# Attention and a two-layer MLP on one core: queries on partitions 0-63, keys on 64-127, transposes and scores on 64-row halves, key tiles of 120, masks multiplied

## The chip, the cores and the metric

The kernel runs on one core of one Trainium2 chip. The metric is the device time of one execution in microseconds; lower is better. An execution that the hardware profiler recorded gives, beside its time, the start and end of every instruction on the engines: PE (TensorE: matmuls, with PEld for its weight loads), DVE (VectorE), ACT (ScalarE), POOL (GpSimd) and SP (SyncE, which issues DMAs here). ACT and POOL issue DMAs too. A "q" behind an engine's name (SPq) is its sequencer, which issues.

## The reference, cut to what matters

`q`, `k`, `v` are [4, 8, 768, 64] in fp32 (batch, head, token, dimension). Heads 0, 2 and 6 are "retrieval" heads with a full causal mask; the other five are "stream" heads, which see the first 4 keys and a window of 64.

```
scores = scale * np.matmul(q, k.transpose(0, 1, 3, 2))
stream_keep = causal & (is_sink | in_win)      # n_sink = 4, window = 64
mask   = causal for retrieval heads, stream_keep for stream heads
a      = softmax(where(mask, scores, -1e9))
x      = (a @ v) as [3072, 512]                # heads side by side
h      = x @ w_in                              # [3072, 2048]
out    = (max(h, 0) + alpha * min(h, 0)) @ w_out    # [3072, 512]
```

## The kernel before, in words

**Segments.** The 32 heads are worked off in 16 segments `n`, two heads `hh` each: four segments per batch, with the head pairs of `PAIRS` = (2, 6), (1, 5), (0, 4), (3, 7). So n = 0, 4, 8, 12 hold two retrieval heads, n = 2, 6, 10, 14 one retrieval and one stream head, the others two stream heads. The MLP works on token tiles `t` (two per batch, 512 and 256 tokens): P1 (`w_in`, L510), relu on ACT (L515) and prelu on DVE (L522), P2 (`w_out`, L530), and output rows by way of `ot`.

**The order is written out.** `ORDER` (L14-72) lists every step by name; the loop at L672 emits them one after the other, and each engine's queue runs its own instructions in that order. Names: L load, C cast to bf16, T transpose, t copy of the transposed q or k out of PSUM, S scores, s exp, m mask multiply, A attention times V, a normalise, X and x transpose of the result and its copy, P p g O o the MLP, wi and wo weight loads, warm dummy matmuls. Segments n = 0 to 3 (batch 0) come ahead of the MLP: this is called the ramp here. From then on attention of the next batch is mixed with the MLP of the one before.

**Loads.** q and k of one head are 192 KB, on 128 partitions with six token rows each (L186, L189: packets of 1,536 bytes). V of a retrieval head goes to 128 partitions (L201). V of a stream head is laid out in seven overlapping key tiles: KEYS = 124 keys on partitions 4 to 127 (L206), and the four sink keys on partitions 0 to 3 of every tile (L209), in packets of 256 bytes. All of these are issued by SP in their order, but for one k load on ACT. The weights are issued by POOL with a cast (L576, L580).

**From load to scores.** Each head's q and k are cast to bf16 (L276, 128x384 each), most on POOL, in its queue's order. Pairs of bf16 dimensions are taken as one fp32 word and transposed on PE, three 128x128 transposes for q and three for k of a segment (L308). `put_q` copies q to `qT` (128 rows: head 0 on rows 0-63, head 1 on 64-127), `put_k` copies each head's keys to its own `kT`, whose other 64 rows are zero (filled at the start). Because of those zeros a score matmul can use all 128 rows (L352 in batch 0, L362 later). From n = 4 on, scores wait in a list `burst`; when both heads have at least SPLIT = 576 columns in it, they are issued in 64-row form instead, alternating between the halves (L369).

**Masks.** In batch 0 the mask is added inside PE's accumulation: a matmul of an identity with a table of 0 and -30000 (L400, L430). From n = 4 on, the exponentials are multiplied by a 0/1 mask on DVE (L415 `mr` for retrieval heads, L450 and L453 `ms` for stream heads).

**After the scores.** ACT takes the exponential into `eR` or `eS` (L407, L441, L444); PE multiplies with V and a column of ones (L467); DVE normalises into `xn` (L476, L477); three fp32 transposes per segment (L485) and a DVE copy (L490) put the result into `xT`, which P1 reads.

Of the kernel before, what the change touches and what calls it, by code (L numbers as in the profile page):

```python
# [14 lines left out]
busy Lq0.0 warm4 kz0 warm5 one nms id Lk0 zero nmr Lq0.1 Lk3 warm0 warm8 Cq0.1 Ck0.0 Tk0.0 Cq0.0 Tq0.0 kz2 qz0 Tq0.1  # L15
Ck0.1 Ck3.0 nma Tk0.1 Lk1 Lq1 Ck3.1 idb Lk2 tk0.0 kz3 Ck1.1 Ck1.0 warm6 tq0.1 tq0.0 S0.0.1 tk0.1 Tk3 tk3.0 tk3.1
S0.1.1 s0.1.1 warm2 s0.0.1 Cq1 La Tk1 kz1 tk1.0 S0.1.2 sz0 s0.1.2 warm7 Tq1 vo S0.0.0 Lq3 s0.0.0 Ck2.1 S0.1.0 s0.1.0
Ck2.0 Cq3 tq1 S1.0.0 tk1.1 Tk2 S1.1.0 Lv0 s1.0.0 s1.1.0 Tq3 Cv0 Lq2 tq3 S1.1.1 A0.1 m4.0.2 s1.1.1 S0.0.2 s0.0.2 S1.0.1
s1.0.1 Cq2 sz1 tk2.0 Al al Lv1 Cv1 tk2.1 Tq2 wi0 a0.1 wi1 A0.0 a0.0 S3.0.0 A1.0 s3.0.0 S3.0.1 s3.0.1 tq2 vz Lv2 Lv3
A1.1 S3.1.1 s3.1.1 S3.1.0 s3.1.0 S2.0.0 a1.1 a1.0 X1 wi2 S2.0.1 Cv3.0 s2.0.0 x1 sz2 s2.0.1 Cv3.1 wi3 wi7 X0 x0 S2.0.2  # L20
s2.0.2 A3.0 S2.1.0 warm3 s2.1.0 wi6 a3.0 Cv2 A2.0 a2.0 S2.1.1 A3.1 P0.0.0 a3.1 s2.1.1 A2.1 a2.1 P0.1.0 X3 m8.1.2 x3
P0.3.0 m12.1.2 X2 x2 P0.4.0 Lq4 P0.5.0 P0.3.1 Lq5 P0.6 p0.6 m6.0.2 g0.6 P0.1.1 P1.6 P0.0.1 p1.6 Lk4 wi5 P0.3.2 p0.3
g0.3 Cq4 P0.0.2 p0.0 g1.6 P0.5.1 P0.5.2 p0.5 P0.7 g0.5 wi4 P1.2 g0.0 P0.4.1 P0.4.2 p0.4 g0.4 P0.13 Lk5 p0.13 g0.13
p0.7 P1.14 p1.14 P0.14 g1.14 p1.2 P1.0 Cq5 g0.7 Tq4 Ck4.1 p1.0 P0.12 tq4 p0.14 g0.14 P0.1.2 g1.0 P0.2.0 P0.2.1 Ck4.0
Tk4 P1.8 tk4.0 P0.11 tk4.1 P0.2.2 P0.8 Lq6 wo0 g1.2 P1.12 wo1 p0.1 g0.1 p0.11 m4.1.2 p0.12 g0.12 p0.8 g0.8 p1.12
S4.1.4 p1.8 g0.11 s4.1.4 g1.8 P1.10 Ck5.1 Tq5 P0.10 Lk6 p0.10 g0.10 P0.9 tq5 g1.12 P0.15 p0.9 Ck5.0 g0.9 Lk7 Tk5 Ck7.1
p0.15 P1.4 Ck7.0 O1.1.0 Cq6 p0.2 p1.4 O1.0.0 g0.2 O0.2.0 tk5.0 tk5.1 g0.15 O0.0.0 Lq7 Cq7 p1.10 g1.4 Tq6 S4.1.2 s4.1.2
Ck6.0 tq6 g1.10 S4.0.4 O1.0.1 O0.2.1 O1.1.1 wo2 s4.0.4 S4.0.3 S4.1.0 s4.0.3 Tk7 tk7.0 wo3 O0.2.2 O1.0.2 Lv5 tk7.1
s4.1.0 Ck6.1 Tk6 ns Tq7 tq7 O0.0.1 O0.0.2 tk6.0 tk6.1 O0.2.3 S5.1.1 Cv5 s5.1.1 m5.1.1 O0.0.3 o0.2 S5.0.0 S5.1.0 m4.1.4
S5.0.2 S5.1.2 S5.0.1 s5.1.0 m5.1.0 s5.1.2 O1.0.3 S4.1.3 s5.0.1 m5.0.1 s4.1.3 m4.1.0 m4.1.3 O0.3.0 O0.3.1 Lv7 Cv7  # L30
s5.0.2 Lv6 s5.0.0 m5.0.0 S7.0.1 S7.1.0 o1.0 S7.1.2 m5.0.2 S7.0.0 o0.0 A5.0 m5.1.2 s7.0.0 a5.0 s7.0.1 m4.0.3 O1.1.2
A5.1 m7.0.1 S7.0.2 O0.3.2 m4.0.4 s7.1.0 Lk9 Ck9.0 s7.1.2 S4.1.5 S4.0.2 S4.0.0 S4.1.1 s7.0.2 S4.0.1 Ck9.1 O0.3.3 a5.1
s4.1.5 s4.1.1 Lv4 s4.0.1 S7.1.1 s7.1.1 m7.0.0 X5 Cv6 m4.1.5 s4.0.2 m7.0.2 A7.0 s4.0.0 m7.1.0 Cv4 O1.1.3 m4.1.1 S4.0.5
o1.1 a7.0 m4.0.1 O0.1.0 m7.1.2 m4.0.0 x5 s4.0.5 o0.3 S6.0.5 m4.0.5 A4.0 S6.0.1 S6.1.1 m7.1.1 s6.0.1 A7.1 a4.0 S6.0.0
S6.1.0 a7.1 S6.0.3 s6.1.1 A4.1 m6.1.1 Lk8 s6.0.5 S6.1.2 a4.1 s6.0.3 m6.0.3 Ck8.0 Ck8.1 Tk8 Lq9 Lq8 Cq8 O0.1.1 S6.0.4
m6.0.1 S6.0.2 s6.0.0 m6.0.0 X4 s6.1.2 Lk12 m6.1.2 m6.0.5 s6.1.0 s6.0.4 O0.1.2 m6.1.0 A6.1 s6.0.2 m6.0.4 Lv8 x4 a6.1
A6.0 X7 a6.0 O0.1.3 x7 X6 Tq8 Cq9 Tq9 x6 Tk9 P2.1 tq8 Lk10 P2.8 p2.1 g2.1 Lk11 Ck11.1 P2.14 tq9 p2.14 Cv8 P2.5 g2.14
p2.8 g2.8 P2.2 Lq11 P2.9 Lq10 P2.11 tk9.0 p2.2 g2.2 p2.9 g2.9 o0.1 tk8.0 tk8.1 P3.14 tk9.1 P2.12 p2.12 p3.14 Lq12
g3.14 P2.15 Ck10.0 P2.0 p2.11 g2.11 p2.0 Cq10 p2.5 Tq10 tq10 Cq12 g2.12 P2.3 p2.3 g2.0 P2.13 g2.3 p2.13 g2.13 P2.6
P2.7 Lq13 g2.5 p2.7 S8.0.4 s8.0.4 P2.4 g2.7 p2.6 P3.10 g2.6 p3.10 Lq14 p2.4 g2.4 Ck11.0 Tk11 p2.15 Lk15 Cq11 Tq11 P3.2  # L40
g3.10 p3.2 g3.2 P3.8 P3.4 p3.4 g3.4 O2.1.0 p3.8 P2.10 p2.10 P3.6 O2.1.1 g2.10 O2.1.2 g2.15 O2.1.3 Lv11 Cv11 o2.1 Lv9
tk11.0 tk11.1 tq11 p3.6 S8.1.1 s8.1.1 g3.6 P3.12 O2.0.0 g3.8 P3.0 p3.0 O2.0.1 O2.0.2 O2.0.3 g3.0 Lv10 S9.0.0 S9.1.1
S9.1.2 p3.12 g3.12 S9.0.2 S9.0.1 S9.1.0 O2.3.0 O2.3.1 o2.0 s9.0.1 s9.1.0 s9.1.2 s9.1.1 S8.1.5 S8.1.3 S8.0.3 S8.0.1
Ck10.1 Lk14 s9.0.2 s8.1.5 s8.1.3 Tk10 tk10.0 tk10.1 Cq13 Ck12.0 s8.0.1 m8.0.1 m8.1.3 O2.3.2 O2.3.3 S8.1.0 m8.1.1
S8.0.5 s9.0.0 m8.1.5 m9.0.0 S8.0.2 S8.1.2 S8.0.0 S8.1.4 m9.0.2 m10.0.2 m9.1.0 m8.0.4 s8.0.3 m9.1.2 s8.1.0 s8.1.4
m8.1.4 s8.0.2 s8.0.0 s8.0.5 O3.0.0 O3.0.1 S11.1.0 Cv9 O3.0.2 Lv15 m9.1.1 A9.1 m9.0.1 A9.0 s11.1.0 S11.0.0 s8.1.2
s11.0.0 m8.1.0 m8.0.0 O3.0.3 o3.0 m8.0.5 m8.0.3 A8.0 a9.1 S11.1.2 S11.1.1 S11.0.2 S11.0.1 o2.3 s11.0.1 Cv10 A8.1
s11.1.1 s11.0.2 a9.0 X9 a8.0 O3.1.0 a8.1 x9 S10.0.5 S10.1.2 s11.1.2 S10.0.4 S10.1.1 S10.0.0 m11.1.2 O3.1.1 m11.1.1
Ck12.1 Tk12 Lq15 m11.0.1 m11.1.0 s10.1.2 Lk13 s10.1.1 s10.0.0 X8 m10.1.1 Tq12 tq12 m11.0.2 m10.1.2 A11.1 a11.1 O2.2.0
S10.0.1 s10.0.4 Lv12 s10.0.5 tk12.0 tk12.1 O3.1.2 S10.1.0 Ck13.0 S10.0.3 S10.0.2 m10.0.4 m11.0.0 m10.0.5 m10.0.0  # L50
# [12 lines left out]
s14.1.2 s12.0.4 m12.0.4 m12.0.5 S12.1.2 s12.1.2 O4.1.2 S14.1.1 m12.1.4 S14.0.5 m12.1.3 S14.0.3 S14.0.0 S14.0.4 S14.1.0
s14.1.0 m14.1.0 s14.1.1 m14.1.1 A12.0 a12.0 s14.0.3 m14.1.2 s14.0.0 A15.1 m14.0.3 s14.0.5 O4.1.3 A12.1 a12.1 A14.1
a14.1 s14.0.4 m14.0.4 S14.0.1 S14.0.2 s14.0.2 O5.0.0 m14.0.5 s14.0.1 m14.0.0 m14.0.1 O5.0.1 a15.1 A14.0 X12 o4.1 X15
O5.0.2 a14.0 X14 x12 x14 O5.0.3 x15 P6.6 p6.6 P7.0 p7.0 g7.0 o5.0 P7.6 P6.14 P7.8 p6.14 g6.14 P6.12 P6.11 p6.11 g6.11
P7.12 p7.12 g6.6 p7.6 P7.10 P6.8 P6.2 g7.6 P6.10 p6.2 g6.2 p6.12 g7.12 P6.0 p6.10 g6.10 P6.3 p6.3 g6.12 g6.3 P6.7 p6.7
p6.0 g6.0 p7.10 g7.10 g6.7 P6.15 P6.5 P6.1 p6.1 p6.8 p7.8 g6.8 g6.1 g7.8 P6.9 P6.13 P6.4 p6.9 P7.2 p6.13 O6.0.0 p6.15
g6.13 g6.15 O6.1.0 p7.2 p6.4 P7.4 O6.3.0 g6.4 g7.2 O7.0.0 P7.14 p6.5 g6.5 O6.3.1 O6.2.0 O6.2.1 g6.9 O6.2.2 O6.2.3 o6.2
O6.0.1 O6.0.2 O6.0.3 o6.0 O6.3.2 p7.4 O6.3.3 o6.3 g7.4 O6.1.1 O6.1.2 O6.1.3 m12.0.2 o6.1 p7.14 g7.14 O7.0.1 O7.0.2  # L70
O7.0.3 m8.0.2 o7.0 L0 l0 L1 l1 L2 l2 warm1
""".split()


@with_exitstack
def kernel(
    ctx: ExitStack,
    tc: tile.TileContext,
    q: bass.AP,
    k: bass.AP,  # L80
    v: bass.AP,
# [18 lines left out]
    PAIRS = [(2, 6), (1, 5), (0, 4), (3, 7)]  # L100
    NSINK = 4
    NT = 7
    KEYS = 124
    WIDE = KEYS + 64
    SLOT = WIDE + 64
    KEY0 = [64 - KEYS + KEYS * j for j in range(NT)]
# [74 lines left out]
    def rows_in(buf):  # L181
        return buf.rearrange("p h i d -> p h (i d)")
# [530 lines left out]
```

## Time and profile before

| what | value |
|---|---|
| median of 3 runs | 252.78 us (252.49 to 253.58) |
| the profiled execution | 250.98 us |
| its span, first to last instruction | 249.2 us |
| granted TensorE clock, mean | 0.978 |
| PE busy | 234.2 us, 94% |
| DVE busy | 157.3 us, 63% |
| ACT busy | 147.9 us, 59% |
| POOL busy | 58.9 us, 24% |
| DMA | 30.34 MB in 43,374 packets, 28,870 of them under 512 bytes |

A page of the profile shows the span in 40 slices of 6.2 us: a digit is the busy share of a slice in tenths. A matmul's end is modelled and lies behind the start of the next one, so a PE that is busy is not PE at its peak; how far one matmul's start is from the next (its pitch) is read from the chain, the view that follows the work that ended last back to its releasers. Groups of instructions give count, busy time and mean duration. Windows give the busy time of every engine in a stretch, then the granted clock, the DMA share and GB/s.

### The profile page before, as it was taken

How to read it: one execution, taken by the hardware profiler on the slowest of the kernel's cores; microseconds unless marked ns; L12 is line 12 of the kernel's file. 1: busy time of each engine (PE TensorE's matmuls, PEld its weight loads, DVE VectorE, ACT ScalarE, POOL GpSimd, SP SyncE). 2: the span in 40 equal slices, each digit the busy share in tenths (PEclk: the TensorE clock that was granted, in tenths of full speed). 3: DMA queues.
4: the chain of work that ended last, by engine and by line, in shares of the span. 5: the costliest groups of instructions: out<-in, count | busy, mean ns of one | idle time of the engine just before them, and what ended most of it. 6: DMA issues, size and time to landing. Idle time of an engine off the chain costs nothing.

```text
span 249.2 us, 5160 instructions
## 1 busy us (share of the span) xinstructions
PE 234.2 (94%) x1961; PEld 147.0 (59%) x1961; DVE 157.3 (63%) x429; ACT 147.9 (59%) x302; POOL 58.9 (24%) x106
## 2 busy tenths in 40 slices
PE   8996259999999999999999999999999999999995
PEld 7785146666555576557545665575455667455444
DVE  4765125678715996886839894988658663885020
ACT  5584310688999883586477745576569624572231
POOL 4944063820011470340040506200011000000000
PEclk9999957999999999999999999999999999999999
DMA  7946769999337969443553943000021111000132
GB/s 219 313 106 113 123 109 265 317 239 180 63 69 199 316 196 277 173 136 72 129 151 82 281 97 122 1 3 0 1 86 43 45 42 45 0 1 3 42 126 84
DMA packets 43374, 30.34 MB, mean 122 GB/s; under 512 B 28870, under 2 KB 41558, under 8 KB 43350
## 3 DMA queue, kind: packets, MB, share of 16 engines
q1 hardware_dynamic: 37158, 20.70, 29.6%
q0 software_dynamic: 5728, 8.91, 15.5%
q10 hardware_dynamic: 464, 0.40, 0.5%
q8 instruction: 15, 0.25, 0.4%
q14 instruction: 9, 0.07, 0.1%
HBM read 27.92 MB, written 6.29 MB: 137 GB/s over the span
## 4 chain that ended last, share of the span: by engine, by line
PE 77%; SPq 10%; DMA 6%; DVE 4%; POOL 1%; issue 1%; ACT 0%; DVEq 0%
PE P L510 32%; PE P L530 29%; SPq L209 6%; PE P L467 5%; DMA vf<-in_v_dram 5%; PE P L308 3%; PE P L369 3%; PE P L362 2%; DMA kf<-in_k_dram 2%; PE P L485 1%; PE P L547 1%; DVE xn L477 1%; SPq L206 1%; DVE eR L415 1%; SPq L201 1%; SPq L189 1%
## 5 line engine op out<-in xcount | busy, mean ns | idle before, releaser
L522 DVE SCALAR_TENSOR_TENSOR g<-neg,oma,P 128x256 bf16<-128x256 f32 (+1 forms) x128 | 71.1, 610 | 39.2 <-ACT neg L515 38.8
L510 PE MATMUL P<-xT,w_in_b 128*128 128x512 bf16 (+1 forms) x512 | 87.9, 327 | 0.0
L530 PE MATMUL P<-w_out_b,g 128*128 128x512 bf16 x368 | 87.8, 379 | 0.0
L515 ACT ACTIVATE neg<-P 128x512 f32<-128x512 f32 x96 | 54.4, 599 | 36.9 <-PE P L510 32.5
L510 PEld LDWEIGHTS <-w_in_b 128*128 128x128 bf16 x512 | 50.0, 98 | 32.3
L530 PEld LDWEIGHTS <-g 128*128 128x128 bf16 x368 | 34.6, 98 | 34.4 <-issue 1.0
L407 ACT ACTIVATE eR<-P 128x448 bf16<-128x448 f32 (+1 forms) x63 | 34.8, 604 | 6.9 <-PE P L400 3.0
L441 ACT ACTIVATE eS<-P 128x376 bf16<-128x376 f32 (+1 forms) x55 | 26.6, 525 | 20.1 <-PE P L430 10.6
L538 POOL DMA_DIRECT2D out_dram<-ot x18 | 11.4, 632 | 94.7 <-ACT ot L536 94.3
L536 ACT COPY ot<-P 128x512 f32<-128x512 f32 x23 | 13.3, 592 | 24.1 <-PE P L530 22.6
L450 DVE TENSOR_TENSOR eS<-eS,ms 128x376 bf16<-128x376 bf16 x45 | 15.8, 368 | 11.5 <-ACT eS L441 11.3
L477 DVE TENSOR_TENSOR xn<-P,rcp 128x384 bf16<-128x384 f32 x32 | 18.9, 591 | 1.1
L467 PE MATMUL P<-vb,eS 128*128 128x65 bf16 x240 | 11.1, 200 | 8.7 <-POOL vb L296 6.5
L467 PEld LDWEIGHTS <-eS 128*128 128x128 bf16 x240 | 10.1, 102 | 11.4 <-issue 8.7
L276 POOL CAST natk<-kf 128x384 bf16<-128x384 f32 x20 | 12.7, 661 | 9.1 <-DMA kf<-in_k_dram 8.7
L276 POOL CAST natq<-qf 128x384 bf16<-128x384 f32 x20 | 11.5, 623 | 8.8 <-DMA qf<-in_q_dram 5.5
L311 ACT COPY qT<-P 128x768 bf16<-128x768 bf16 (+1 forms) x13 | 10.4, 796 | 4.9 <-PE P L308 4.9
L352 PE MATMUL P<-qT,kT 128*128 128x188 bf16 (+6 forms) x68 | 12.2, 261 | 0.6 <-DVE qT L311 0.5
L467 PE MATMUL P<-vb,eR 128*128 128x65 bf16 x252 | 10.1, 197 | 1.1 <-DVE xT L490 1.1
L415 DVE TENSOR_TENSOR eR<-eR,mr 128x128 bf16<-128x128 bf16 x54 | 10.8, 239 | 0.3 <-ACT eR L407 0.2
L467 PEld LDWEIGHTS <-eR 128*128 128x128 bf16 x252 | 9.3, 100 | 2.7 <-DVE xT L490 1.4
L476 DVE RECIPROCAL rcp<-P 128x6 f32<-128x6 f32 x32 | 6.1, 190 | 7.0 <-PE P L467 6.7
(81 smaller groups left out, 208.2 us busy)
## 6 DMA issues: line engine op xcount, KB each, us to landing
kf<-in_k_dram SPq DMA_DIRECT2D x31, 192.0 KB
qf<-in_q_dram SPq DMA_DIRECT2D x15, 384.0 KB
out_dram<-ot POOLq DMA_DIRECT2D x18, 256.0 KB, 2.8
vf<-in_v_dram SPq DMA_DIRECT2D x19, 217.0 KB
vf<-in_v_dram SPq DMA_DIRECT2D x12, 192.0 KB
w_in_b<-in_moe_w_in_dram POOLq DMA_DIRECT2D x8, 256.0 KB, 7.7
w_out_b<-in_moe_w_out_dram POOLq DMA_DIRECT2D x4, 512.0 KB, 11.9
out_dram<-ot SPq DMA_DIRECT2D x5, 256.0 KB
```

Of the source, the lines that this page charges most:

```text
L209: nc.sync.dma_start(dst[0:NSINK, :, hh, :], dram(v, o, [[D, NSINK], [0, NT], [1, D]]))
L276: copy(in_pairs(nat, hh), buf[:, hh].rearrange("p (i t) d -> p i t d", t=2))
L407: nc.scalar.activation(ebuf[n, hh][:, lo:hi].rearrange("p (x c) -> p x c", x=len(parts)), P[:, got[0]:got[0] + len(parts), 0:(hi - lo) // ...
L441: nc.scalar.activation(slots_of(n, hh, m), sc[:, :, 0:2 * WIDE].rearrange("p x (s c) -> p x s c", c=WIDE), AF.Exp, scale=scale)
L450: nc.vector.tensor_tensor(slots, slots, ms[:, 0:2, :] if m == 0 else ms[:, 1:3, :], op=ALU.mult)
L467: nc.tensor.matmul(pav[:, i, :], e[:, o:o + 128], vv[:, j, hh, 0:D + 1], start=(m == 0), stop=(m == len(terms) - 1))
L477: nc.vector.tensor_tensor(in_pairs(xn[n], hh), pav[:, :, :, 0:D], rcp.to_broadcast([128, 3, 2, D]), op=ALU.mult)
L510: nc.tensor.matmul(psg[:, w * i:w * (i + 1)], w_in_b[:, c, 128 * fb:128 * (fb + 1)], xT[:, c, o:o + w], start=(x == 0), stop=(x == 3))
L515: nc.scalar.activation(neg[t, f], bank(held["P", t, f][0]), AF.Relu, scale=-1.0)
L522: nc.vector.scalar_tensor_tensor(g_buf[t % 2][:, fb, 0:w], neg[t, f][:, c], oma[:, fb:fb + 1], bank(got[0])[:, c], op0=ALU.mult, op1=ALU.add)
L530: nc.tensor.matmul(bank(held["O", t, s][0]), g_buf[t % 2][:, f, 128 * s:128 * (s + 1)], w_out_b[:, f, :], start=(f == 0), stop=(f == 15))
L536: nc.scalar.copy(ot, bank(got[0]))
```

## The change

- q and k of a segment share one buffer `qkf`: q on partitions 0-63, k on 64-127, twelve token rows per partition (packets of 3,072 bytes). Each load fills 64 partitions. One cast instruction takes q and k of a head together (128x768).
- The fp32 transposes work on 64 rows and 64 columns: six for q and six for k per segment, q's on rows 0-63 and k's on 64-127, queued in `burst` and issued alternating between the halves. The result's transposes (X) are halved in the same way, into two adjacent banks.
- `kT` holds both heads one below the other, without the zero halves; only the unused columns are zero-filled. All scores, those of batch 0 too, are 64-row matmuls, whatever the burst's size; SPLIT is gone.
- The masks of batch 0 are multiplied after the exponential, as in the later batches; the PE matmuls with the identity and the tables `nmr` and `nms` are gone.
- KEYS is 120 instead of 124: stream V loads go to 120 partitions, and the key tiles hold 4 + 120 rows.
- Names in `ORDER` can carry an engine (`/P`, `/V`, `/A`): 58 of the 118 mask steps are on POOL (49 of them from n = 4 on), 12 of the 23 output copies that ACT had are on DVE, 8 of 16 x copies on ACT, casts on POOL, DVE and ACT.
- `ORDER` as a whole is another one. Its dummy matmuls stand elsewhere: 25 instead of 3 behind the start of the dense MLP.

The core of the diff (`ORDER` and renamed buffers left out):

```diff
-    KEYS = 124
+    KEYS = 120
...
-    qf = [stat.tile([128, 2, 6, 64], fp32, name=f"qf{i}") for i in range(NF)]
-    kf = [stat.tile([128, 2, 6, 64], fp32, name=f"kf{i}") for i in range(NF)]
+    qkf = [stat.tile([128, 2, 12, 64], fp32, name=f"qkf{i}") for i in range(NF)]
...
-    kT_all = stat.tile([128, NK, 2, 7 * 128], bf16, name="kT")
+    kT_all = stat.tile([128, NK, 7 * 128], bf16, name="kT")
...
+    def load_qk(eng, src, at, n, hs):
+        h = heads(n)[hs[0]]
+        dst = qkf[n % NF][at:at + 64, hs[0]:hs[-1] + 1].rearrange("p h i d -> p h (i d)")
+        dims = [[12 * D, 64], [4 * S * D, len(hs)], [1, 12 * D]]
+        eng.dma_start(dst, dram(src, (n // 4 * H + h) * S * D, dims))
...
-            nc.sync.dma_start(dst[NSINK:128, 0:nt, hh, :], dram(v, o + KEY0[0] * D, [[D, KEYS], [KEYS * D, nt], [1, D]]))
+            nc.sync.dma_start(dst[NSINK:NSINK + KEYS, 0:nt, hh, :], dram(v, o + KEY0[0] * D, [[D, KEYS], [KEYS * D, nt], [1, D]]))
...
+    def cast_qk(n, hh, lo, hi, eng):
+        nat[n] = NAT0[n] if n < 4 else NAT[n % 2]
+        src = qkf[n % NF][:, hh, 2 * lo:2 * hi].rearrange("p (i t) d -> p i d t", t=2)
+        cast_of(eng)(in_pairs(nat[n], hh, 6)[:, lo:hi], src)
...
+    def T_pe(n, key):
+        held["q", key] = take(*ANY)
+        held["k", key] = take(*ANY)
+        words = nat[n].bitcast(fp32).rearrange("p (i c) -> p i c", i=6)
+        c = D if key == "0.0" else 128
+        for i in range(6):
+            for half, x in enumerate((held["q", key][0], held["k", key][0])):
+                r = slice(64 * half, 64 * half + 64)
+                queue(half, 128, key, nc.tensor.transpose, bank(x)[0:c, i:i + 379:6], words[r, i, 0:c], ident_f[r, r])
...
+    def queue(half, columns, *rest):
+        burst.append((half, columns) + rest)
+
+    def one_score(n, hh, m, to, keys, queries):
+        own = slice(D * hh, D * hh + D)
+        queue(hh, queries.shape[1], (n, hh, m), nc.tensor.matmul, to, keys[own], queries[own])
 
     def emit_burst():
 
-        halves = [[x for x in burst if x[1] == hh] for hh in range(2)]
-        columns = [sum(x[5].shape[1] for x in half) for half in halves]
-        if min(columns) < SPLIT:
-            for x in burst:
-                nc.tensor.matmul(*x[3:6], start=True, stop=True)
-        else:
...
+        halves = [[x for x in burst if x[0] == half] for half in range(2)]
+        at = [0, 0]
+        while halves[0] or halves[1]:
+            half = min((h for h in range(2) if halves[h]), key=lambda h: at[h])
+            columns, key, fn, *args = halves[half].pop(0)[1:]
+            fn(*args, **({"start": True, "stop": True} if isinstance(key, tuple) else {}))
+            at[half] += max(65, columns) + 5.5
...
-                if n < 4:
-                    nc.tensor.matmul(to, ident, nms[:, min(j, 1), a:z], start=False, stop=True)
...
+    def by(n, hh, m):
+        return {"V": nc.vector, "P": nc.gpsimd}[on(f"m{n}.{hh}.{m}", "V")]
...
-                nc.vector.tensor_tensor(ej, ej, mr, op=ALU.mult)
+                by(n, hh, m).tensor_tensor(ej, ej, mr, op=ALU.mult)
...
-            nc.tensor.transpose(bank(got[0])[:, 128 * i:128 * (i + 1)], words[:, i, :], ident_f)
+            for half, x in enumerate(got):
+                r = slice(64 * half, 64 * half + 64)
+                queue(half, 128, f"x{n}", nc.tensor.transpose, bank(x)[:, 64 * i:64 * (i + 1)], words[r, i, :], ident_f[r, r])
...
-        nc.scalar.copy(ot, bank(got[0]))
+        cast_of(on(f"o{t}.{s}", "A"))(ot, bank(got[0]))
```

## The prediction

> **What bounds the kernel now.** I read the busy shares and the 40 slices first, then the chain of waits, then windows of single stretches (busy time of PE, PEld, DVE, ACT and POOL, clock, DMA share, GB/s).
>
> ```profile
> span 249.2 us, 5160 instructions
> ...
> PE   8996259999999999999999999999999999999995
> ...
> PEclk9999957999999999999999999999999999999999
> DMA  7946769999337969443553943000021111000132
> GB/s 219 313 106 113 123 109 265 317 239 180 63 69 199 316 196 277 173 136 72 129 151 82 281 97 122 1 3 0 1 86 43 45 42 45 0 1 3 42 126 84
> ...
> PE 77%; SPq 10%; DMA 6%; DVE 4%; POOL 1%; issue 1%; ACT 0%; DVEq 0%
> ```
>
> There are two regimes. From slice 8 on PE is full and the clock whole; before that PE has a hole at 25-37 us, with half the clock after it, and the chain there is not PE's (SPq and DMA, 16% of the span). The chain in order of time (start, length, what) gives the seam: dense matmuls start at 42.12 us and end at 246.05. The hole is V arriving, by the chain and by stretches of the windows:
>
> ```profile
> 22.22 5.69 SPq L209
> 28.71 6.71 DMA vf<-in_v_dram
> ...
> 42.12 9.75 PE P L510 x61
> ...
> 242.50 3.55 PE P L547 x48
> ```
> ```profile
> 15.00:18.00 3.00, 3.00 (x53) 2.83 (x51) 1.46 (x5) 2.30 (x6) 1.02 (x2) 1.00 0.31 71
> ...
> 18.70:19.90 1.20, 0.66 (x10) 0.53 (x7) 1.13 (x4) 0.00 (x0) 0.00 (x0) 1.00 0.84 192
> 2.50:10.00 7.50, 7.13 (x66) 5.83 (x63) 4.20 (x15) 3.66 (x5) 6.02 (x17) 1.00 1.02 324
> 35.00:36.00 1.00, 0.37 (x4) 0.10 (x1) 0.48 (x2) 0.78 (x1) 1.00 (x2) 0.50 0.95 129
> 53.00:59.00 6.00, 6.00 (x45) 4.19 (x43) 4.54 (x9) 5.04 (x10) 0.00 (x0) 1.00 1.23 205
> ```
>
> While 124-partition V loads run, 71 GB/s flow at a share of 0.31, a quarter of the 1.23 that a full machine shows: 4 of 16 engines. Around the one 128-partition V load of that stretch (18.7 us) it is 192 at 0.84. I read that a load is dealt in equal parts over as many engines, up to 16, as divide its partitions: 124 = 4 x 31, 128 = 16 x 8. 120 = 15 x 8 would take 15.
>
> In the dense regime, 203.95 us, I priced every PE instruction by its pitch in the chain and counted them in the built program: 512 columns 0.216, 128 columns 0.056, an attention-times-V matmul 0.033 (33 in 1.10), an fp32 transpose 0.109 (9 in 0.98). They sum to 201.8. So PE is within 2.1 us of its own floor: only less PE work, or an earlier start, can move the end. ACT (128.8) and DVE (137.6) have a third free there. Key tiles of 120 leave the columns and the 240 attention-times-V matmuls of stream heads as they were.
>
> **Part 1, dense PE work.**
> - *Transposes.* 108 of 0.109 us = 11.8 become 216 of 64 rows and 64 columns. Half the columns is 0.056; two at a time, 108 x 0.056 = 6.0. No row shows an fp32 one on 64 rows. Bounds: 6.0, and 11.8 if two weight loads can't run together (weight loads in the trace: 141 ns fp32, 98 ns bf16, so fp32 takes at least 43 ns longer, and two in turn come near the 0.109). I take 6.0: the nearest row, bf16 matmuls on 64-row halves, does run two at a time, as below. Saves 5.7.
> - *Scores.* Before, 67 matmuls (15,408 columns) use 128 rows, 6.6 us; 137 are paired in 12 bursts, 6.1 us. After, all 204 (the same 41,472 columns) are in halves; queued as the program has them, unequal halves included, 9.9. Saves 2.8.
> - *Warm-up matmuls.* 25 instead of 3 after the seam: adds 22 x 0.056 = 1.2.
> - *Entering and leaving 64-row form.*
>
> ```profile
> 126.34 0.60 PE P L369 x14
> 126.94 1.83 PE P L530 x8
> ...
> 131.47 0.68 PE P L369 x8
> ```
> The longer halves are 1,152 and 1,344 columns: 0.50 and 0.57 at pitch. So the halves do run together, and each burst costs 0.10 more. After has 36 runs of 64-row work for 12: adds 24 x 0.10 = 2.4.
> - The floor goes 201.8 to 194.5 (-5.7 - 2.8 + 1.2), switches 1.2 to 3.6.
>
> **Part 2, the ramp.** The masks added by PE (53 matmuls) and halved scores cost nothing there: PE had waits of 6.5 and 2.1 us for `vb`. What counts is when data and masks are ready.
> - *q and k.* Same bytes, but each load fills 64 partitions. In the before order 3.3 MB land by 12.5 us (219, then 313 GB/s). By that rate the 13th load, k2.1, which POOL's first big cast needs, lands at 10.1. The nearest row with 64 partitions is w_in at 35-36 us: 129 GB/s against 205 for w_out, 0.63; by it 10.1 becomes 15.0 (data flow from 1.8). One row shares queue and packet kind, the other the partitions: I take the middle, 12.6, and keep both ends.
> - *V.* 1.7 MB: 25 us before (from 10 to 35.4, where the chain's DMA piece ends), with 1 MB of weights between. Bounds: unchanged, or all at 192 GB/s, 9. I take the second, as 15 of 16 engines. SP's wait goes too: the sink load after each (L209) held SP 2.9 to 5.7 us, its minimum is 0.30. V then lands at about 24, no longer last.
> - *What is late next: POOL.* Its queue now carries casts of 128x768, mask multiplies and the w_in issues, all in order. A 768 cast lies between 0.83 (contiguous `vb` row) and 1.24 (two of the 0.62 strided): 1.1. A two-input multiply is not in the trace on POOL; for 368 columns between 0.5 (copies, 0.8 ns per column and 0.2) and 1.24 (two strided casts): 0.85; so 0.4 for 128, 1.2 with its short tail, 1.5 for 736. From 12.6: two casts of n=2, one V cast, four multiplies, one cast of n=3: 5.7. Two multiplies, m1.0.0, V cast, m1.0.1, last cast of n=3, two w_in issues: 6.5, so 24.8. m2.1.1, w_in, two V casts: 3.0. Then m3.1.0, m3.1.1, m3.0.1: 3.9, 31.7. Those masks were additions inside PE's accumulation; now exp, multiply and AV stand in line, and POOL's lateness is PE's. Then AV 0.5, reciprocal and scaling 0.9, X 0.5, x copy 0.6, hand-overs 0.6: dense at 34.8, 7.3 earlier. ACT's queue (nine exps of 896 columns at 0.9, the stream exps 7.5, copies and casts 5: some 20 us from 8.5) ends near 29 and hides under it. If PE idles ahead of the seam its clock is halved, as now (two 512-column matmuls took 0.85 us at 39.2, 0.43 at 40.6): up to 1.5 more, within the range.
> - *Kept at nothing:* the smaller zero fills (1.6 on DVE, 1.7 on ACT, 0.8 on POOL before), as their engines idle on data; without that cover 1 us. The tail: same three cuts, 3.15 us.
>
> **Part 3, elsewhere in the dense part.** 49 mask multiplies go to POOL (39 us busy of 204), some output copies to DVE, some x copies to ACT. By row prices DVE gains about 6, ACT 11, POOL 26 over the run, below 70% each. Other waits were 0.9; I put 2.5, for multiplies late on POOL, where they stand behind casts and output issues that wait for `ot`.
>
> **Sum.** 34.8 + 194.5 + 3.6 + 2.5 + 3.15 = 238.6 for a span of 249.2. The profiled execution took 250.98, 1.8 around the span: 240.4. The three runs' median is 252.78, 0.7% above that execution; scaled, **242.1**.
>
> **Weighed against the skill.** The Trainium skill ("DMA: Bandwidth & Descriptors", Why a DMA increments its semaphore by 16 and not by 1) says the engine count is the largest number up to 16 that divides both slowest dimensions; the shares above agree for 124 and 128, and 120 then takes 15. The Trainium skill ("SBUF — State Buffer", Door 1: The DMA port swizzle) speaks against the change: partitions 0-63 reach half of the ports, 196 GB/s against 328 at 1 MiB, and loads to the two halves don't add up. By that ratio q and k land as in the first rival below; by the q/k row, as in my lower end. The w_in row leans to the page, but is one microsecond with other loads beside it.
>
> **Rivals.**
> - *Half-filled loads are slow.* q/k at 0.63: POOL starts 2.4 later, dense 37.2: 244.5. For: the w_in row. If q and k in one queue fill both halves together: 239.6.
> - *fp32 weight loads don't pair.* Transposes stay 11.8: +5.8, 248. For: the 141 ns; against: only that bf16 pairs do.
> - *120 partitions don't spread.* V still lands at 35, dense at 42: 249.4. Against: the two shares.
> - *POOL becomes the bound, slower than before.* Each of 24 dense heads must have its last multiply before AV. The gain is 10.7; it is gone if every head stalls PE 0.45 us beyond my 2.5 in all, and 0.5% slower from 0.5 us a head. At 1 us: 266. For: POOL's cast of `natk` reaches 1257 ns against 622, and DVE's multiply 710 against 347, so the two engines do hold each other up; two-input multiplies on both would meet oftener. Against: a third of DVE and over half of POOL is free, and dense heads have MLP matmuls between.
>
> **How the numbers follow.** Forecast (242, give or take 4): 0.47. Slow half loads, full price: 0.16. Unpaired weight loads: 0.22. V not spread: 0.05. POOL as bound: 0.10, of it 0.07 slower by 0.5%, 0.03 within. A run-to-run change under 0.5% can't be told from none here. Low end: cheap POOL prices (0.5 for 368 columns, 0.83 a cast: 5 us off the queue), q/k at full rate and no other waits give 232. High end: slow loads with unpaired weights, 250.3. Range 232 to 251. Faster 0.90, same 0.03, slower 0.07.
>
> **What would show it.** V: GB/s near 200 in slices 3 and 4, the sink loads' issues near 0.3 us. Seam: the first long run of L491 (P1's matmul after the change) near 35. Pairs: 12 transposes of a segment in about 0.35 us of chain (0.65 if unpaired). Switches: PE gaps of 0.1 at each 64-row burst. POOL: PE or AV waits that name `eS` or `eR` on POOL; if these exceed 10 us in the dense part the prediction is wrong.

## The result, and the profile after

The changed kernel takes **259.92 us** (median of 4 runs, 259.09 to 260.42); the kernel before, run beside it, 252.63. The ratio is 1.0282, 95% interval 1.0237 to 1.0326: 2.8% slower, where 242.1 us was forecast. The profiled execution took 260.3 us with a span of 258.6; the prediction's sum for that span was 238.6. So 20.0 us are to be found. Some executions of a kernel take 1.5% or more longer than its fastest one; the ratios and intervals leave those out.

The page of the changed kernel, the same lines that were shown of before:

```profile
span 258.6 us, 5351 instructions
...
PE   6777859999999969989989799999999999999994
...
PEclk9555555999999997999999999999999999999999
DMA  6999999999861215995931994100021102000024
GB/s 170 222 214 180 233 225 209 244 202 192 192 161 44 84 43 133 225 181 101 196 110 41 224 199 104 43 1 0 4 81 41 43 4 81 3 0 0 0 75 171
...
PE 69%; DMA 13%; DVE 8%; POOL 5%; issue 2%; SPq 1%; ACT 0%; DVEq 0%; POOLq 0%
```

Three things are to be seen. The hole at 25-37 us is gone, but PE's row of nines begins in the seventh slice, as before. The DMA row is at 9 from slice 2 to slice 10, yet GB/s stay at 180 to 244 where before had 313 in its second slice: the engines are busy and move less. And the chain now holds DVE 8% and POOL 5%, with PE slices of 6 to 8 in what was a solid row of nines.

The chain in order of time (start, length, what) up to the seam:

```profile
7.91 6.48 DMA qkf<-in_k_dram
...
14.50 0.99 POOL g L266
...
20.71 1.53 POOL eS L426
...
25.22 0.73 POOL w_in_b L557
25.95 13.19 DMA w_in_b<-in_moe_w_in_dram
...
39.28 2.29 PE P L491 x5
...
42.09 8.34 PE P L491 x39
```

V is not in it any more. POOL starts on k2.1 at 14.5, where the prediction had 12.6, and is through with its first two w_in issues at 26.6, where the prediction had 24.8: late by its start. But w_in then needs 13.2 us to land, and PE stands and waits for it:

```profile
PE P L491 <- DMA w_in_b<-in_moe_w_in_dram: 3.6, 1, 3.6
```

So the dense part starts at 42.1, where before it started at 42.12. In windows (busy time of PE, PEld, DVE, ACT, POOL, then clock, DMA share, GB/s):

```profile
4.00:10.00 6.00, 3.08 (x40) 2.26 (x39) 2.58 (x8) 2.67 (x3) 1.07 (x3) 0.80 1.06 228
...
16.00:24.00 8.00, 6.90 (x76) 5.24 (x76) 7.77 (x21) 5.65 (x11) 7.80 (x12) 0.50 1.12 193
...
29.00:36.00 7.00, 6.50 (x90) 5.23 (x87) 5.81 (x14) 4.09 (x8) 6.60 (x9) 0.50 1.15 225
36.00:42.00 6.00, 2.72 (x11) 0.98 (x11) 0.54 (x1) 0.10 (x1) 5.14 (x8) 0.50 1.19 216
```

A packet of q or k (3,072 bytes) takes 121 ns while few are under way, at 2-3 us, and 231 ns at 4-10 us (medians). Half-filled loads thus occupy all 16 engines at 228 GB/s. Each of them also holds SP's queue for 0.60 us, where a load of the same bytes on 128 partitions held it for 0.43 in before. While w_in is under way (29-36 us) the share is 1.15: the next batch's q and k, which SP now reaches at 23-27 us because no V load holds it, run beside it.

For the dense part I took the distance from each PE instruction's start to the next one's and compared it with the sum by pitch:

| | before | after |
|---|---|---|
| seam to last matmul's start | 204.0 | 212.6 |
| sum by pitch | 201.8 | 194.4 |
| above the sum | 2.2 | 18.2 |
| runs of 64-row work | 12 | 36 |

What PE waited for there (engine, line, releaser: total, times, longest); the same view of before names none:

```profile
PE P L444 <- POOL eS L426: 1.5, 2, 1.4
PE P L444 <- DVE eR L391: 1.3, 1, 1.3
PE P L444 <- DVE ot L517: 0.7, 1, 0.7
PE P L491 <- DVE g L503: 0.7, 1, 0.7
PE P L444 <- DVE eS L426: 0.6, 1, 0.6
PE P L444 <- DVE vb L271: 0.3, 1, 0.3
PE P L336 <- DVE qT L284: 0.2, 1, 0.2
```

L444 is attention times V: it waits for masks, on POOL and on DVE, and for what stands ahead of them on DVE. The groups of the 128-column multiply, of before:

```profile
L415 DVE TENSOR_TENSOR eR<-eR,mr 128x128 bf16<-128x128 bf16 x54 | 10.8, 239 | 0.3 <-ACT eR L407 0.2
```

and of after, on POOL and on DVE:

```profile
L391 POOL TENSOR_TENSOR eR<-eR,mr 128x128 bf16<-128x128 bf16 x38 | 16.3, 450 | 5.4 <-ACT eR L379 5.2
L391 DVE TENSOR_TENSOR eR<-eR,mr 128x128 bf16<-128x128 bf16 x34 | 15.4, 494 | 0.5 <-ACT eR L379 0.4
```

The same instruction on DVE takes twice as long. Those that overlap no POOL computation average 235 ns (13 of 34), those that do 654 (21). One such place, DVE's and then POOL's timeline (start, length):

```profile
83.88 1.79 DVE L391 TENSOR_TENSOR eR<-eR,mr 128x128 bf16<-128x128 bf16 x2
85.59 1.42 DVE L271 CAST vb<-vf 128x768 bf16<-128x768 f32 x1
```
```profile
84.25 0.94 POOL L271 CAST vb<-vf 124x896 bf16<-124x896 f32 x1
85.13 0.62 POOL L519 DMA_DIRECT2D out_dram<-ot  x1
85.77 1.52 POOL L391 TENSOR_TENSOR eR<-eR,mr 128x128 bf16<-128x128 bf16 x3
```

Two multiplies of 0.22 each take 1.79, and a V cast that took 0.55 in before takes 1.42 beside POOL's three multiplies.

### The profile page after: what moved, and what is told of

The parts are those of the page before. It is cut to its first block, busy times and chain, and to the rows that moved or that the text cites. A ratio compares the mean times of both kernels' runs of the same rounds, so it can differ in the third digit from the quotient of the medians.

```text
span 258.6 us, 5351 instructions
## 1 busy us (share of the span) xinstructions
PE 237.7 (92%) x2058; PEld 139.2 (54%) x2058; DVE 167.6 (65%) x372; ACT 147.5 (57%) x295; POOL 86.2 (33%) x140
## 3 DMA queue, kind: packets, MB, share of 16 engines
q0 software_dynamic: 5728, 8.91, 14.8%
## 4 chain that ended last, share of the span: by engine, by line
PE 69%; DMA 13%; DVE 8%; POOL 5%; issue 2%; SPq 1%; ACT 0%; DVEq 0%; POOLq 0%
PE P L491 30%; PE P L511 28%; DMA qkf<-in_k_dram 8%; PE P L336 6%; DMA w_in_b<-in_moe_w_in_dram 5%; PE P L444 4%; DVE eR L391 3%; DVE eS L426 1%; POOL eR L391 1%; DVE vb L271 1%; PE P L528 1%; POOL g L266 1%; SPq L185 1%; DVE ot L517 1%; POOL eS L426 1%
## 5 line engine op out<-in xcount | busy, mean ns | idle before, releaser
L426 POOL TENSOR_TENSOR eS<-eS,ms 128x368 bf16<-128x368 bf16 (+1 forms) x27 | 25.9, 967 | 47.2 <-ACT eS L415 47.1
L379 ACT ACTIVATE eR<-P 128x448 bf16<-128x448 f32 (+1 forms) x63 | 34.8, 608 | 7.5 <-PE P L336 4.4
L415 ACT ACTIVATE eS<-P 128x368 bf16<-128x368 f32 (+1 forms) x55 | 26.8, 517 | 16.6 <-PE P L336 12.7
L336 PE MATMUL P<-qT,kT 64*128 64x128 bf16 (+7 forms) x272 | 25.5, 278 | 2.1 <-ACT qT L284 1.0
L336 PEld LDWEIGHTS <-kT 64*128 64x128 bf16 x272 | 14.3, 103 | 12.7 <-issue 8.7
L426 DVE TENSOR_TENSOR eS<-eS,ms 128x368 bf16<-128x368 bf16 (+1 forms) x28 | 14.8, 534 | 8.6 <-ACT eS L415 8.3
L391 POOL TENSOR_TENSOR eR<-eR,mr 128x128 bf16<-128x128 bf16 x38 | 16.3, 450 | 5.4 <-ACT eR L379 5.2
L444 PE MATMUL P<-vb,eS 124*128 124x65 bf16 x240 | 13.0, 208 | 3.4 <-POOL eS L426 1.5
L444 PEld LDWEIGHTS <-eS 124*128 124x128 bf16 x240 | 10.8, 107 | 7.1 <-POOL eS L426 3.0
L517 ACT COPY ot<-P 128x512 f32<-128x512 f32 x11 | 6.5, 592 | 14.2 <-PE P L511 14.2
L517 DVE COPY ot<-P 128x512 f32<-128x512 f32 x12 | 8.3, 688 | 9.3 <-PE P L511 6.6
L444 PE MATMUL P<-vb,eR 128*128 128x65 bf16 x252 | 12.1, 206 | 2.0 <-DVE eR L391 1.5
```

What stands on the lines that cost most here:

```text
L336: fn(*args, **({"start": True, "stop": True} if isinstance(key, tuple) else {}))
L379: nc.scalar.activation(ebuf[n, hh][:, lo:hi].rearrange("p (x c) -> p x c", x=len(parts)), P[:, got[0]:got[0] + len(parts), 0:(hi - lo) // ...
L391: by(n, hh, m).tensor_tensor(ej, ej, mr, op=ALU.mult)
L415: nc.scalar.activation(slots_of(n, hh, m), sc[:, :, 0:2 * WIDE].rearrange("p x (s c) -> p x s c", c=WIDE), AF.Exp, scale=scale)
L426: by(n, hh, m).tensor_tensor(slots, slots, ms[:, first:first + 2 * len(x), :], op=ALU.mult)
L444: nc.tensor.matmul(pav[:, i, :], e[0:rows, o:o + 128], vv[0:rows, j, hh, 0:D + 1], start=(m == 0), stop=(m == len(terms) - 1))
```

## The experiments

Theory: the ramp is lost to half-filled loads, which fill the DMA engines' time so that w_in lands late; the dense part is lost to 64-row switches that were priced at half, and to DVE and POOL holding each other up. Rivals: the loads are hidden and POOL's queue sets the seam; the order itself puts masks too late; the 64-row form alone makes up the 18 us. Seams below are the start of the seventh P1 matmul (before 41.95, after 42.42).

### The ramp

**Spreading V alone.** In before's `load_v`:

```diff
-            nc.sync.dma_start(dst[NSINK:128, 0:nt, hh, :], dram(v, o + KEY0[0] * D, [[D, KEYS], [KEYS * D, nt], [1, D]]))
+            for lo, hi in ((0, 112), (112, KEYS)):
+                nc.sync.dma_start(dst[NSINK + lo:NSINK + hi, 0:nt, hh, :],
+                                  dram(v, o + (KEY0[0] + lo) * D, [[D, hi - lo], [KEYS * D, nt], [1, D]]))
```

> The kernel before, with each stream head's V load cut into two DMAs of 112 and 12 partitions (112 = 16 x 7), nothing else: the spreading of V alone. Theory (V on 4 engines is what makes the hole at 25-37 us): while V flows the 256-byte packets go from about 280 to over 600 a microsecond, the wait for vb ends near 24 instead of 35.4, and the seam comes at 33 to 36 instead of 42.0, so 244 to 247 us. Rival (as in the changed kernel: once SP is free, loads of the next batch and w_in meet, and something else ends last): V lands early too, but the seam stays within 1.5 us of 42, 251 to 254 us.

Measured: **243.2 us**, ratio 0.9602 (0.9527 to 0.9678), seam 36.2. That is the theory's case, a little beyond its 244. The page of this kernel (its profiled execution took 246.1 us, more than its median):

```profile
PE   7999199999999999999999999999999999999994
...
GB/s 218 324 166 154 250 267 298 203 197 190 273 62 89 86 246 274 110 177 141 46 156 273 146 3 87 0 3 0 1 89 43 46 43 46 1 0 3 43 129 86
```

The hole of four slices has shrunk to one. The dense part of this execution (204.7) is that of before, so the 4.8 us by which its span is shorter are ramp; the executions near the median have no trace. The prediction's reading of V was right, and one edit of `load_v` makes a kernel faster than both.

**Half-filled loads in before.** Each q and k load cut into two of 64 partitions (rows 0-63, 64-127).

> The kernel before, with every q and k load cut into two DMAs of 64 partitions each (0-63, 64-127), the same bytes in the same 1,536-byte packets: half-filled loads alone. Theory (a load that fills 64 partitions flows at some 0.6 of the rate): GB/s at 3 to 10 us falls from 313 to about 220 and the q/k of the ramp land some 5 us later, near 17 instead of 12.5. Rival (two loads in flight on the two halves fill all ports together): rate within 10% of before. The time itself should move less than 2 us either way, since V (35.4) stays last.

Measured (one execution): 261.66 us, seam 50.9. It does not answer its question. Packets still took 65 ns, as in before, but only 104 started per microsecond instead of 208: with twice as many DMAs of half the size, SP's issue of 0.60 us each (0.43 for a load on all 128 partitions) was the limit, and V came later behind them. The next run asks it without that.

**Full loads in after.** The rows of q and k land in mixed places, so this kernel does not compute attention.

```diff
-        dst = qkf[n % NF][at:at + 64, hs[0]:hs[-1] + 1].rearrange("p h i d -> p h (i d)")
-        dims = [[12 * D, 64], [4 * S * D, len(hs)], [1, 12 * D]]
+        dst = qkf[n % NF][:, hs[0]:hs[-1] + 1, at * 6 // 64:at * 6 // 64 + 6].rearrange("p h i d -> p h (i d)")
+        dims = [[6 * D, 128], [4 * S * D, len(hs)], [1, 6 * D]]
```

> The changed kernel, with each q and k load written across all 128 partitions (six rows of 256 B in each, q in the first half of a partition's space, k in the second) instead of 64 partitions of twelve rows: the same loads, bytes, order and waits, but the rows of q and k land in mixed places, so what is computed from them is not attention. Theory (a load that fills 64 partitions takes its packets twice as long, 231 ns against 121 alone, all 16 engines are then busy, and w_in, the next batch's q/k and V share what is left): packets of 1,536 B take 65 to 80 ns, k2.1 lands near 10 instead of 14.3, and the seam moves from 42.4 to 35-38: 252 to 256 us. Rival (the ramp is set by POOL's queue and the exp-multiply-AV chain, whatever the loads do): seam within 1.5 us of 42.4, 258 to 260 us.

Measured: **252.09 us**, ratio to before 0.9954 (0.992 to 0.9987), 7.8 less than the changed kernel; seam 34.5. Its windows:

```profile
4.00:10.00 6.00, 4.85 (x56) 3.56 (x55) 3.60 (x12) 3.56 (x5) 1.14 (x3) 1.00 0.99 329
...
16.00:24.00 8.00, 6.20 (x71) 4.83 (x69) 7.57 (x24) 5.99 (x12) 8.00 (x11) 0.50 1.05 262
```

With the same share of the engines' time, 329 GB/s flow instead of 228, and the seam falls on the 34.8 of the prediction. The theory holds: what cost the ramp is how the loads fill the partitions, not their bytes or the order. Two things change along with the partitions. SP's issues take 0.43 us again, so that k2.1 is issued 1.4 us earlier and cast 3.5 us earlier, at 11.0. And the packets are half as large; that their size alone slowed them is not likely, since one of 3,072 bytes took 121 ns while few were under way, no more than two of 65. P1 still waits for w_in once behind the seam (1.2 us).

**w_in earlier.** In after's ORDER, `wi0 wi1` ahead of `C2.1.0`.

> The changed kernel, with the first two w_in loads issued on POOL ahead of its first 768-column cast of segment 2 (about 14.5 us) instead of at 25-26 us. Theory (w_in, which lands at 39.1 beside the next batch's q/k loads, is what holds the seam at 42.4): w_in lands by 25, the seam moves to 37-39, and 255 to 257 us. Rival (the masks on POOL, done at 34.9, with the exp, AV and X behind them hold it as well, or w_in now delays k3): seam within 1 us of 42.4, 259 to 261 us.

Measured: 263.94 us, ratio 1.0459 (1.04 to 1.0519). The first P1 matmuls start earlier (seam 40.1), but k2.1 reached POOL at 16.9 instead of 14.5, the masks came later, and the third w_in load, issued behind them, ran from 37.25 to 48.6. The theory's time fell, and so did the rival's; nearest to what happened is the rival's "or w_in now delays k3", though it was k2.1 that came late, and it was dearer than either said. Moving a load forward moves the shortage to another load while the engines' time is full.

**The next batch's loads out of the way.** `load_qk` of segments 4 to 7 on `nc.scalar`.

> The changed kernel, with the q/k loads of segments 4 to 7 issued from ACT's queue at their place in the order, behind the exps of the ramp, instead of from SP's, which runs ahead to them at 23-27 us. Theory (w_in, issued at 25-26, lands at 39.1 only because these loads, twice as long on half the partitions, share the engines with it): w_in lands by 32, the seam moves from 42.4 to 37-40, 255 to 258 us. Rival (V of segment 3 and q/k of the ramp itself hold w_in, or the masks on POOL, done at 34.9, hold the seam): seam within 1.5 us of 42.4, 258.5 to 262 us.

Measured: seam **37.7**, as the theory says; time 281.88 us, ratio 1.1181 (1.1136 to 1.1226), far outside what either side expected. From its chain:

```profile
35.79 1.40 PE P L491 x5
...
51.87 19.16 DMA vf<-in_v_dram
```

With these loads away w_in is there when P1 first asks, at 35.8: they make 4.7 of the 7.6 us by which the seam came later than the prediction's 34.8. But from ACT's queue they come so late that batch 1 then waits for them (the chain has 6.8 us of `qkf` at 39, then the 19 us of `vf`). They cannot simply be put off.

**The spreading undone.** After with `KEYS = 124`.

> The changed kernel with key tiles of 124 again, so that a stream head's V load covers 124 partitions: the spreading of V undone. Theory (V is on the critical path of the ramp here too, and 4 engines take it 2.5 times as long): V lands after 35, the seam goes from 42.4 to 45-50, 262 to 268 us. Rival (the ramp is set by the sum of all loads on the engines, and V on 4 engines leaves the others to q, k and w_in): seam within 2 us of 42.4, 258 to 262 us.

Measured: **290.66 us**, ratio 1.1537 (1.1505 to 1.1569), seam 52.3, and 38.7 us above the sum by pitch in the dense part. Worse than the theory's 268. In its windows:

```profile
24.00:30.00 6.00, 2.22 (x28) 1.97 (x29) 2.65 (x11) 2.60 (x6) 4.69 (x8) 0.51 0.67 94
29.00:36.00 7.00, 0.00 (x0) 0.00 (x0) 1.01 (x2) 0.00 (x0) 0.00 (x0) 0.50 0.76 113
```

PE stands still for seven microseconds. So key tiles of 120 are worth some 31 us to the changed kernel; without them the other edits would be far slower.

### The dense part

**64-row scores alone.** Before with `SPLIT = 0`.

> The kernel before, with all scores of the dense part in 64-row form (36 runs of 64-row work instead of 12, as many as in the changed kernel's dense part; PE's sum by pitch falls by 1.1 us): the price of entering and leaving 64-row form alone. Theory 1 (0.10 to enter and 0.10 to leave, as gaps of 0.095 ahead of each run and 0.105 within it say): 24 x 0.20 = 4.8, less 1.1: dense part 3.7 us longer. Theory 2 (the prediction's 0.10 in all): 1.3 us longer. Time 256.4 or 254.0 against 252.7.

Measured: 255.73 us, ratio 1.0111 (1.0069 to 1.0153). The dense part is 207.6 for a sum by pitch of 200.65: 7.0 above it instead of 2.2, 4.74 for 24 more runs, **0.20 each**. Theory 1 holds. In the changed kernel's chain a run looks like this:

```profile
63.01 0.97 PE P L491 x4
63.98 0.52 PE P L336 x12
64.51 2.69 PE P L511 x12
```

Four P1 matmuls take 0.86 elsewhere; the four ahead of the run take 0.97. That gap of 0.095 at the entrance is what the prediction left out; it had only the 0.105 within the run. The 12 transposes take 0.52, less 0.105 within the run: 0.41 instead of 0.34 at pitch. They do run two at a time.

**Multiplies on POOL alone.** Before, with the 49 multiplies of segments 4 to 15 that the changed kernel has on POOL put on `nc.gpsimd`.

> The kernel before, with the same 49 mask multiplies of segments 4 to 15 on POOL as in the changed kernel, nothing else: multiplies on POOL alone. Theory (POOL's two-input multiplies take 0.42 and 0.88 us where DVE's take 0.24 and 0.35, hold DVE up meanwhile, and AV waits): DVE's 128-column multiply rises from 239 ns to 350-500, waits of 4 to 10 us in the dense part, 256 to 262 us. Rival (DVE relieved of 15 us makes up for it): 251 to 254 us.

Measured: **262.12 us**, ratio 1.037 (1.032 to 1.0421). The dense part is 11.3 us above its sum instead of 2.2. Its groups:

```profile
L425 POOL TENSOR_TENSOR eR<-eR,mr 128x128 bf16<-128x128 bf16 x32 | 14.3, 464 | 2.8 <-PE P L477 1.6 <-ACT eR L407 0.9
...
L425 DVE TENSOR_TENSOR eR<-eR,mr 128x128 bf16<-128x128 bf16 x22 | 11.2, 544 | 0.6 <-ACT eR L407 0.5
```

DVE has 32 fewer of these multiplies and spends 11.2 us on the rest instead of 10.8 on all. This one part alone makes the kernel before slower by more than the whole change does.

**Taken back in after.** Four kernels that take parts of it back:

- the 49 multiplies on DVE (`/P` dropped from their names)

> The changed kernel, with the 49 mask multiplies of the dense part (segments 4 to 15) that it gives to POOL put on DVE, in the same places of the order. Theory (DVE and POOL hold each other up, so that AV waits for multiplies): DVE's 128-column multiply falls from a mean of 494 ns back to about 240, its V casts from 1150 to about 650, the dense part loses 8 to 12 of its 18.2 us above the floor, 248 to 252 us. Rival 1 (AV waits because the order puts the multiplies too late, whatever engine does them; DVE just gets 16 us more): 258 to 264 us. Rival 2 (the excess is the price of the 36 runs of 64-row work): 258 to 261 us.

- the same, and the 12 output copies on ACT

> The changed kernel, with the 49 multiplies of the dense part on DVE (as in e4) and the 12 output copies that it gives to DVE back on ACT: 8.3 us less on DVE than e4, 7 more on ACT. Theory (in e4 DVE itself is the bound in the attention stretches, 80-100 and 145-150 us, so the waits stayed): the part above the floor falls from 17.4 us in e4 to 12-14, 254 to 256 us. Rival (what is left are places in the order, with POOL's 768-column casts holding DVE up; the copies don't matter): 16 us or more, 258 to 261 us.

- the first, with POOL's casts of 768 columns in halves

> e4 (all dense multiplies on DVE), with each 768-column q/k cast that POOL does in the dense part cut into two of 384 columns, 0.5 instead of 1.0 us each, the size that the kernel before uses. Theory (what is left of AV's waits in e4 are DVE multiplies held for as long as a POOL instruction lasts: 1.06 to 1.95 us at 76.7, 83.8, 85.7 and 94.6, where POOL casts 768 columns): these fall to 0.7-1.0, the part above the floor from 17.4 us to 14-16, 256 to 258.5 us. Rival (DVE has too much to do in these stretches whatever POOL does, or a hold lasts until POOL's whole queue is empty): 17 us or more, 259 to 261 us.

- the first, with those casts on ACT

> e4 (all dense multiplies on DVE), with the eight 768-column q/k casts that POOL does in the dense part given to ACT at the same places of the order; POOL keeps two V casts and its DMA issues there. Theory (in e4 and e12 the multiplies on DVE are held through a run of POOL's casts, however they are cut: 1.6 to 1.95 us at four places): DVE's 128-column multiply falls from 333 to 230-260 ns and the part above the floor from 17.4 us to 12-15, 254 to 257 us; ACT's 1.3 us a cast costs little of it. Rival (the stretches of attention are too dense in DVE and ACT work as they are ordered, and POOL is not the reason any more): 17 us or more, 259 to 263 us, with the multiplies short all the same.

| | after | multiplies on DVE | + copies on ACT | + short casts | + casts on ACT |
|---|---|---|---|---|---|
| median of the runs, us | 259.92 | 259.64 | 259.57 | 259.14 | 265.05 |
| ratio to before | 1.0282 | 1.0285 | 1.0292 | 1.0245 | 1.0498 |
| half width of its interval | 0.0045 | 0.006 | 0.0037 | 0.0038 | 0.0042 |
| dense part above the sum by pitch, us | 18.2 | 17.4 | 17.4 | 17.5 | 22.7 |
| of it ahead of AV | 5.6 | 4.3 | 4.1 | 4.1 | 1.3 |
| of it ahead of scores and transposes | 3.9 | 4.7 | 4.9 | 4.7 | 10.2 |

My expectation for the first (8 to 12 us back) fell, and so did those for the copies and for short casts. The multiplies got shorter (494 to 333 ns on average), but the held ones are still there, and short casts do not shorten them. DVE and POOL in the kernel with short casts:

```profile
78.05 1.83 DVE L392 TENSOR_TENSOR eR<-eR,mr 128x128 bf16<-128x128 bf16 x1
```
```profile
77.63 2.16 POOL L267 CAST nat<-qkf 128x384 bf16<-128x384 f32 x4
```

One multiply is held until four casts in a row are through. With the casts on ACT, AV's waits do go (1.3 us) and the multiplies fall to 295 ns, the direction that the theory gave; but the casts then stand among the exponentials, scores and transposes wait instead, and it is slower. Both sides are partly right: POOL's work holds DVE up, and in this order neither DVE nor ACT could take that work over without a loss elsewhere.

**All engines as before, in after.** Suffixes dropped for segments 4 to 15 and all output copies.

> The changed kernel, with the work of the dense part (segments 4 to 15 and all output copies) back on the engines that the kernel before uses: multiplies on DVE, output copies on ACT, q/k casts on POOL, x copies on DVE. PE's instructions and the order are unchanged. Theory (AV, P1 and score waits of some 8 us come from DVE's and POOL's load in the attention stretches, and what remains of the 18.2 us above the floor is 36 runs of 64-row work at 0.10 to enter and 0.10 to leave, 7.2, transposes 1.5 and the cold clock 1.3): excess 10 to 12, 251 to 254 us. Rival (the order itself puts the multiplies and copies too late): 258 to 262 us.

Measured: 271.14 us, ratio 1.0726 (1.0663 to 1.0789), 29.6 above the sum by pitch. The rival is nearer, though the time is beyond it too: this order with other engines is worse. PE's longest waits there are those of AV for stream masks on DVE (5.0 us in five waits). It says nothing more on the hold-up.

## Why the prediction was wrong

The 20.0 us, by its own terms: the seam 7.6 (34.8 became 42.4), switches 3.6, waits 7.2, the slow clock at the seam's start 1.3 (kept in the range, not in the sum), the tail 0.4; the excess of 0.1 is rounding. The waits are a remainder: the 18.2 us above the sum, less 36 switches and the slow clock, leave 9.7, of which 2.5 were in the sum. No one of these terms alone takes the time out of the stated range of 232 to 251; the seam's 7.6 would have made it 249.7.

- **Part 1, the floor: right.** 194.4 by the recount for 194.5. Transposes pair; the rival that they don't is out.
- **Part 1, entering and leaving 64-row form: mis-sized.** 36 runs at 0.10 were put in; 0.20 is the price, 7.2 in all. The gap ahead of a run lay in before's "other waits", where I did not look for it. With it, the floor's 7.4 us gain shrinks to 2.6 before anything waits.
- **Part 2, q and k: the step that failed.** "I take the middle, 12.6": k2.1 was cast at 14.5, near the upper end. I had weighed the w_in row down as one "with other loads beside it"; that was misread, since all 126 packets that start in that microsecond are w_in's. The larger error is the kind of price: I charged a half-filled load as a delay of its own landing. It is a charge on all 16 engines: batch 0's 1,024 packets of 231 ns make 14.8 us of 16 engines, where 2,048 of 65 ns made 8.3 (medians). I asked for V and POOL what comes late next, but never for w_in, which I had landing in time at no cost. Two runs split the 7.6 us: with the next batch's loads away from w_in the seam is at 37.7, near the 37.2 that the first rival gave for slow half-filled loads, and the other 4.7 are w_in's. The run with full loads puts the seam at 34.5, so the rest of Part 2 stands, with some luck: k2.1 was cast at 11.0 there instead of 12.6, and POOL's queue to the last mask was 20.1 us long instead of 19.1.
- **What I had weighed against it.** The Trainium skill ("SBUF — State Buffer", Door 1: The DMA port swizzle) gives 196 GB/s for 64 partitions against 328 for 128. The Trainium skill ("SBUF — State Buffer", "Can I just issue two DMAs to hit both halves?") says that loads to the two halves don't add up. Here it was 228 against 329 GB/s, with q's and k's loads under way together: the trace agrees. I had weighed it and then taken a middle value.
- **Part 2, V: right,** and worth more than the 7.3 us that I gave the whole ramp: 9.5 us alone in before, some 31 in after.
- **Part 2, POOL's prices: right** (0.99 for a cast of 768, 0.39 to 0.45 for 128, 0.92 for 368, 1.58 for 736); the masks of n = 3 were done at 34.9 instead of 31.7, 1.9 of it by the later start, the rest by a queue that took 20.4 us instead of 19.1.
- **Part 3, waits of 2.5: the second failure.** 9.7 us were lost to waits, slower restarts after them and transposes. The mechanism was in the last rival: POOL's work holds DVE up and AV waits. I had set it at 0.10 because a third of DVE was free on average. In the attention stretches it was not (time held up counts as busy here): at 80-90 us of before DVE is busy 9.47 of 10, and at 90-100 us of after 8.77, with POOL at 8.20. That POOL's multiplies cost this much is shown in before alone (9.3 us); in after, moving them back to DVE returns 0.3 us, since POOL's casts still hold DVE up and other waits come in their place. How the 9.7 us divide between the hold-up and the order stays open.
- **What each part does.** V spread: 9.5 us gained alone. Half loads: 7.8 lost (after against the run with full loads). POOL's multiplies: 9.3 lost alone in before. 64-row scores: 3.0 lost alone. These were measured in different kernels and need not add up. Another order for the same parts was not tried.

## What to carry to other kernels

A load that uses half of the partitions is to be priced as engine time that every other load lacks, not as its own lateness; then ask for each load behind it. Count the price of a change of form, in and out (0.20 us here), for every run of it, against what the form saves. Before work is put on an engine that is idle on average, look at the stretches where it will run and at which other engine it holds up there; and try the one part that the profile points at by itself, as here V's load, before a whole redesign.

## What the runs showed of the hardware that was not expected

- A two-input multiply on DVE waits for more than one POOL instruction: 1.83 us through four casts in a row, 217 ns where POOL computes nothing. The Trainium skill ("SBUF — State Buffer", Who interferes with whom) says that the second to come is blocked until the first finishes; here it outlasted the first by three.
- Cutting POOL's casts in half left the waits where they were (17.4 and 17.5 us above the sum).
- A load on 64 partitions held SP's queue for 0.60 us, one on 128 partitions for 0.43, whether the 64-partition load had the same bytes (after) or half of them (the halved loads in before).
- The clock row of a page can miss a slow stretch. In the kernel with multiplies on DVE and copies on ACT it shows whole clock throughout:

```profile
PEclk9999999999999999999999999999999999999999
```
```profile
39.55 2.29 PE P L490 x5
```

Yet its first five P1 matmuls take the same 2.29 us as in after, where the row has half clock, and start 0.38 to 0.43 us apart, where the sum by pitch has 0.216. What the half clock costs the ramp therefore stays open: no run of the changed kernel is known to have had the whole clock there.
